# One of four token groups: turned by 32x32 blocks on VectorE through device memory, instead of by TensorE into PSUM

## The chip, the cores and the metric

The kernel runs on one core of a Trainium2 chip. A core has five engines that work side by side, each through its own queue in order: TensorE (PE in the profile; its weight loads are shown as PEld), VectorE (DVE), ScalarE (ACT), GpSimd (POOL) and SyncE (SP), which here only issues transfers. Engines wait for each other by semaphores. SBUF is the on-chip memory that transfers and engines read and write, PSUM the small one into which TensorE writes. The metric is the device time of one execution in microseconds; less is better.

## What is computed

A lightning-attention layer (causal attention with a decay per head, in blocks) for 4 sequences of 768 tokens, 8 heads of 64; its output x (4 x 768 x 512) goes through a Fourier mix and a two-layer MLP:

```python
def _moe_ref(x, w_ch1, w_ch2):
    X = np.fft.fft(x, axis=1)
    X = np.fft.fft(X, axis=2)
    mixed = np.real(X).astype(np.float32)
    u = x + mixed
    mu = np.mean(u, axis=-1, keepdims=True)
    var = np.mean((u - mu) ** 2, axis=-1, keepdims=True)
    un = (u - mu) / np.sqrt(var + 1e-06)
    ch = np.maximum(un @ w_ch1, 0.0) @ w_ch2      # 512 -> 2048 -> 512
    return (u + ch).astype(np.float32)
```

All is in fp32.

## The kernel before

**Groups.** The tokens of a sequence b are six tiles of 128. After the mix, they are handled as three groups g of two tiles each (G = 2, 256 tokens), a tile of the first half of the sequence and one of the second. `ORDER` lists the groups as they come: for each b, g = 1, 2, 0. The first four, `PLAIN` = (0, 1), (0, 2), (0, 0), (1, 1), go through the MLP by plain matrix products. The last eight, `LATE`, go through it two groups at a time at the end of the kernel, by products of combined quarter matrices (`combine_weights`, `late`), which need fewer matmuls.

**Stages.** `attn(b)` computes the attention of sequence b chunk by chunk; `fft_ln(b)` mixes it by matmuls with cosine and sine tables, adds x, and calls `norm` for each group. Beside the first two sequences the MLP's weights are loaded and decoded (`load_weights`, lines 205 to 225: the inputs are 64-bit floats, and ScalarE and VectorE make fp32 of them). `mlp(b, g, f0, f1)` does one plain group for the hidden columns f0 to f1: the first layer (line 636) into the PSUM pool pm (3 banks), relu copies to SBUF (lines 642 and 644), the second layer (line 650), then the sum with u. The first three plain groups are done in two halves of the hidden columns, all first halves (while the weights' second half is still coming) before the second halves; the fourth is done whole after them. `weave` and `beside` emit the instructions of `front` (attention and mix) and `mlp` in turns; from this order as a priority, a scheduler of the framework makes each engine's queue, with a model of durations and of free buffers. So the order on an engine is the program's order only in part.

**norm(g)**, the function that is changed: mean and variance by VectorE (546, 547), 1/sqrt by GpSimd (550, 551), then for each of the two tiles the normalised tokens `un` (563, 564), which have to be turned, so that the 512 features lie across partitions. There are two ways.
- A plain group: four TensorE transposes (569) into a PSUM tile of the pool pa (5 banks, which attention and mix use as well), and one ScalarE copy (573) into `ut`, a tile of the pool up. There are three buffers for ut, and each is free again when the second half of its group has read it for the last time.
- A late group: VectorE transposes each 32x32 block (577) into a tile of the pool ep (tag e, two buffers, shared with the weight decode's e), and four transfers on SP's queue put the blocks in their places in a device-memory tile `utd` (581). The rows u go to device memory too (587), which frees their x buffers; `late` loads both later.

A plain group's rows u stay in their x buffers until its MLP is done.

**The tail.** After `fr` and most of `back` have been emitted, `front_end.close()` gives the front's SBUF back, `combine_weights(0)` makes the combined matrices on VectorE (700), and `late` follows, four times two groups, until the end.

The lines that matter to the change: 551 to 587 (norm), 629 to 664 (mlp), 205 to 225 (the other user of e), 852 to 868 (the order of halves and the tail).

Of the kernel before, what the change touches and what calls it, by code (L numbers as in the profile page):

```python
# [76 lines left out]
def kernel(  # L77
# [10 lines left out]
    nc = tc.nc  # L88
# [8 lines left out]
    KO = DM // 128  # L97
# [5 lines left out]
    G = 2  # L103
# [14 lines left out]
    def plain_pool(name, bufs):  # L118
        return plain_end.enter_context(tc.tile_pool(name=name, bufs=bufs, side="right"))
# [9 lines left out]
    up = plain_pool("up", 3)  # L129
# [9 lines left out]
    def new(pool, shape, tag, **kw):  # L139
        cnt[0] += 1  # L140
        return pool.tile(shape, F32, tag=tag, name=f"{tag}{cnt[0]}", **kw)

    def psum_a(shape):
        return new(pa, shape, "pa")
# [265 lines left out]
    uts, utd, ud = {}, {}, {}  # L410
# [45 lines left out]
    def fold_a(b):  # L456
        for a, n in enumerate(BLK):
            yield from fold_x(b, a, n, 1, eo[b][a][1][0:n, 1, 0:DM], xn_[b, HC + a][0:n])
# [32 lines left out]
    def fft_ln(b):  # L491
        sets = []

        def piece(a, i, n):

            c0 = W + QM if i == 4 else QM * (i % 2)
            return sets[a][i in (2, 3)][0:BLK[a], n, c0:c0 + (1 if i == 4 else QM)]

        if b in LEADS:
            yield from fold_a(b)  # L500
            yield from fold_b(b, sets)
            yield 2.0
        else:
            yield 1.0
            run(fold_a(b))
            yield 6.0 if b - 1 in LEADS else 3.0
            run(fold_b(b, sets))
            yield 12.0 if b - 1 in LEADS else 9.0


        for i in range(5):
            ps = psum_a([128, 2, NK])
            m = 128 if i < 4 else 1
            for n in range(2):
                for a, rows in enumerate(BLK):
                    mm = nc.tensor.matmul(ps[0:m, n, :], lhsT=piece(a, i, n), rhs=cs[0:rows, a, i in (2, 3), n, :],  # L516
                                          start=(a == 0), stop=(a == 1))
                    if i + n + a == 0:
                        tc.keep_in_program_order(mm)
            nc.scalar.copy(ys[i][0:m, 0:2 * NK].rearrange("p (k n) -> p n k", n=2), ps[0:m])  # L520
            yield 1.4


        def width(t, ps, only_a):
            y = [ys[i][:, 128 * t:min(128 * t + 128, S // 2 + 1)] for i in range(5)]
            ps = ps[0:1] if only_a else ps
            mm = nc.tensor.matmul
            if not only_a:
                mm(ps[:, HM + QM:DM], lhsT=y[2], rhs=dt[:, 2, 0:QM], start=True, stop=True)
            mm(ps[:, HM:HM + QM + 1], lhsT=y[0], rhs=dt[:, 0, :], start=True, stop=False)  # L530
            mm(ps[:, HM:HM + QM + 1], lhsT=y[4], rhs=dt[:, 4, :], start=False, stop=True)
            mm(ps[:, 0:QM], lhsT=y[1], rhs=dt[:, 1, 0:QM], start=True, stop=True)
            if not only_a:
                mm(ps[:, QM:HM], lhsT=y[3], rhs=dt[:, 3, 0:QM], start=True, stop=True)

        def even_odd(t):
            return t.rearrange("p (m r) -> p r m", r=2)

        def halves(t):
            return t.rearrange("p (r k) -> p r k", r=2)  # L540

        def norm(g):
            mv = new(np_, [128, G, 2], "mv")
            for i in range(G):
                stt = new(np_, [128, 6], "stt")
                nc.vector.bn_stats(stt, xs[b, TT[g][i]])  # L546
                nc.vector.bn_aggr(mv[:, i, :], stt)
            ve = new(np_, [128, G], "ve")
            rs = new(np_, [128, G], "rs")
            nc.gpsimd.tensor_scalar(ve, mv[:, :, 1], EPS, None, op0=ALU.add)  # L550
            nc.gpsimd.tensor_tensor(rs, ve, mhalf, op=ALU.pow)

            yield 9.0 if (b, g) == PLAIN[0] else 1.0
            plain = (b, g) in PLAIN
            if plain:
                ut = uts[b, g] = new(up, [128, KO, G * 128], "ut")
            else:

                to = utd[b, g] = dram.tile([128, KO, G * 128], F32, name=f"utd{b}{g}")
            for i in range(G):  # L560
                un = new(np_, [128, DM], "un", bufs=1)
                u = xs[b, TT[g][i]]
                for o, x in ((un[:, 0:HM], u[:, 0:HM]), (un[:, HM:DM], u[:, DM - 1:HM - 1:-1])):
                    nc.vector.tensor_scalar(o, x, mv[:, i, 0:1], rs[:, i:i + 1],
                                            op0=ALU.subtract, op1=ALU.mult)
                if plain:
                    pt = psum_a([128, KO, 128])
                    for c in range(KO):
                        mm = nc.tensor.transpose(pt[:, c, :], un[:, 128 * c:128 * c + 128], ident)
                        if (b, g, i, c) == (*PLAIN[0], 0, 0):  # L570

                            tc.keep_in_program_order(mm)
                    nc.scalar.copy(ut[:, :, 128 * i:128 * i + 128], pt)
                else:

                    uq = new(ep, [128, DM], "e")
                    nc.vector.transpose(uq, un)
                    for r in range(0, 128, 32):
                        dst = to[:, :, 128 * i + r:128 * i + r + 32].rearrange("(a d) c n -> d c a n", d=32)
                        src = uq[r:r + 32].rearrange("p (c a n) -> p c a n", c=KO, n=32)  # L580
                        nc.sync.dma_start(dst, src)
                yield 0.7
            if plain:
                return
            for T in TT[g]:
                ud[b, T] = dram.tile([128, DM], F32, name=f"ud{b}{T}")
                nc.sync.dma_start(ud[b, T], xs.pop((b, T)))

        for t in (1, 2, 0):
            ps = psum_a([128, DM])  # L590
            width(t, ps, False)

            A = halves(ps)[:, ::-1, 0:QM]
            B = bs[t % 2]
            nc.scalar.copy(B[:, 1:HM:2], ps[:, QM:HM])
            nc.scalar.copy(B[:, 2:HM:2], ps[:, HM + QM + 1:DM])
            ds = new(fp, [128, 2 * (HM + 2)], "ds")
            nc.scalar.copy(ds[:, HM:2 * HM + 2:HM + 1], ps[:, HM + QM:HM + QM + 1].broadcast_to([128, 2]))
            nc.vector.tensor_tensor(even_odd(ds[:, 0:HM]), A, even_odd(B[:, :]), op=ALU.subtract)
            nc.vector.tensor_tensor(even_odd(ds[:, HM + 1:2 * HM + 1]), A, even_odd(B[:, :]), op=ALU.add)  # L600
            u, v_ = xs[b, t], xs[b, HC + t]
            nc.vector.tensor_tensor(halves(u), halves(u), halves(ds)[:, :, 0:HM], op=ALU.add)
            nc.vector.tensor_tensor(halves(v_), halves(v_), halves(ds[:, 1:DM + 1])[:, ::-1, :], op=ALU.add)
            yield 1.6
            if t == 0:
                ps = psum_a([128, DM])
                width(HC, ps, True)
                x3 = xn_.pop((b, HC))
                nc.vector.tensor_tensor(even_odd(v_[0:1, 0:HM]), halves(ps[0:1])[:, ::-1, 0:QM],
                                        even_odd(x3[0:1, 0:HM]), op=ALU.add)  # L610
                nc.vector.tensor_tensor(v_[0:1, HM:DM:2], ps[0:1, 0:QM], x3[0:1, HM:DM:2], op=ALU.add)
                nc.vector.tensor_tensor(v_[0:1, HM + 1:DM:2], ps[0:1, HM + 1:HM + QM + 1],
                                        x3[0:1, HM + 1:DM:2], op=ALU.add)
                yield 0.9
            yield from norm(t)
# [3 lines left out]
    PLAIN, LATE = ORDER[:4], ORDER[4:]  # L619

    def store(b, T, y, cols=slice(0, DM)):
        if T < HC:
            nc.sync.dma_start(out[b, 128 * T:128 * T + 128, cols], y[:, cols])
        else:
            nc.gpsimd.indirect_dma_start(out=out.rearrange("b s d -> (b s) d"),  # L625
                                         out_offset=row_of(2 + HC * (b + 1) + T - HC),
                                         in_=y[:, :], in_offset=None)

    def mlp(b, g, f0=0, f1=FO):

        ut = uts[b, g]
        hr = []
        for fc in range(f0, f1):
            ps = psum_m([128, G * 128])
# [186 lines left out]
    def run(gen):  # L821
        return sum(gen)
# [27 lines left out]
    run(beside(mix, 24.0, beside(att1, 2.75 * t_chunk, w, 0.16 * NW), 0.16 * NW + 1.75 * t_chunk))  # L850

    half = [[mlp(b, g, h * FO // 2, (h + 1) * FO // 2) for b, g in PLAIN[:3]] for h in range(2)]
    fr = chain([att1, fft_ln(1)] + [front(b) for b in range(2, B)])
    t_rest, t_back = 3 * t_front - 5 * t_chunk, len(PLAIN) * t_mlp - 50.0
# [51 lines left out]
```

## Time and profile before

| | us |
|---|---|
| runs: median of 4 (lowest, highest) | 822.75 (822.21, 823.99) |
| the profiled execution | 823.16 |
| its span, first to last instruction | 821.4 |
| granted TensorE clock, mean over the span | 0.998 |
| attention, mix, plain MLP and weight decode together | 0 to 430 |
| the late groups, about 97 for each two | 430 to 821.4 |

In the profile an instruction is named by engine, line and operation, with what it writes and reads (`pm<-ut,w`: a tile of pm out of ut and w). An fp32 matmul appears as two instructions, so the 64 first-layer products of a whole group, 16 by 4, appear as 128; a transpose appears once. "Idle before" is the time for which the engine stood before an instruction, with what ended it. The ends of matmuls are modelled and overlap the next one's start; the starts show the pace. In the list of windows the numbers after a stretch are its length, the busy time of PE, PEld, DVE, ACT and POOL with instruction counts, then the granted clock, the share of the transfer engines' time and GB/s.

### The profile page before, as it was taken

How to read it: one execution, taken by the hardware profiler on the slowest of the kernel's cores; microseconds unless marked ns; L12 is line 12 of the kernel's file. 1: busy time of each engine (PE TensorE's matmuls, PEld its weight loads, DVE VectorE, ACT ScalarE, POOL GpSimd, SP SyncE). 2: the span in 40 equal slices, each digit the busy share in tenths (PEclk: the TensorE clock that was granted, in tenths of full speed). 3: DMA queues.
4: the chain of work that ended last, by engine and by line, in shares of the span. 5: the costliest groups of instructions: out<-in, count | busy, mean ns of one | idle time of the engine just before them, and what ended most of it. 6: DMA issues, size and time to landing. Idle time of an engine off the chain costs nothing.

```text
span 821.4 us, 11694 instructions
## 1 busy us (share of the span) xinstructions
PE 796.2 (97%) x4608; PEld 635.8 (77%) x4608; DVE 438.0 (53%) x1018; ACT 186.3 (23%) x448; POOL 84.5 (10%) x102
## 2 busy tenths in 40 slices
PE   6889899999999999999999999999999999999998
PEld 5767767767585857768648888888888888888886
DVE  6899798766743661355895541265313661146311
ACT  3655344225420211222102200022001210022100
POOL 3123340011021010220100000000000000000000
PEclk9999999999999999999999999999999999999999
DMA  9969524249741126530351011100111001010010
GB/s 238 269 127 281 163 90 129 62 114 208 194 124 51 55 54 136 130 121 26 91 143 62 1 53 51 52 1 0 65 40 52 0 1 39 33 33 0 1 39 26
DMA packets 126684, 68.88 MB, mean 84 GB/s; under 512 B 111150, under 2 KB 112174, under 8 KB 126630
## 3 DMA queue, kind: packets, MB, share of 16 engines
q1 hardware_dynamic: 121488, 55.67, 26.7%
q0 software_dynamic: 2112, 6.69, 2.4%
q10 hardware_dynamic: 3030, 5.78, 1.9%
q8 instruction: 36, 0.59, 0.3%
q14 instruction: 18, 0.15, 0.1%
HBM read 48.72 MB, written 19.40 MB: 83 GB/s over the span
## 4 chain that ended last, share of the span: by engine, by line
PE 80%; DVE 9%; DMA 4%; issue 4%; ACT 1%; POOL 1%; SPq 0%; POOLq 0%; DVEq 0%; ACTq 0%
PE p L770 24%; PE p L723 24%; PE pm L650 10%; PE pm L636 8%; PE pa L332 3%; PE pa L516 3%; PE pa L298 2%; DMA x<-xb,ix 2%; PE pa L328 2%; DMA raw<-in_moe_w_ch_dram 1%; PE pa L274 1%; PE pa L315 1%; PE pa L348 1%; PE pa L279 1%; DVE stt L546 1%
## 5 line engine op out<-in xcount | busy, mean ns | idle before, releaser
L636 PE MATMUL pm<-ut,w 128*128 128x256 f32 x512 | 119.2, 382 | 0.0
L650 PE MATMUL pm<-w,hr 128*128 128x512 f32 x256 | 116.0, 598 | 0.2 <-DVE w L225 0.2
L636 PEld LDWEIGHTS pm<-ut,w 128*128 128x128 f32 x512 | 94.4, 190 | 15.4 <-issue 3.6
L723 PE MATMUL p<-ur,w 128*128 128x256 f32 x384 | 93.8, 379 | 0.0
L650 PEld LDWEIGHTS pm<-w,hr 128*128 128x128 f32 x256 | 46.9, 191 | 49.6 <-issue 48.1
L723 PEld LDWEIGHTS p<-ur,w 128*128 128x128 f32 x384 | 73.0, 190 | 10.3 <-issue 0.5
L723 PE MATMUL p<-us,w1s 128*128 128x256 f32 x256 | 65.7, 379 | 0.0
L770 PE MATMUL p<-w,hs 128*128 128x256 f32 x256 | 58.0, 379 | 0.5 <-DVE y L791 0.5
L770 PE MATMUL p<-w,ha 128*128 128x256 f32 x256 | 57.9, 379 | 0.0
L770 PE MATMUL p<-w2s,hs 128*128 128x256 f32 x256 | 57.9, 379 | 0.0
L770 PEld LDWEIGHTS p<-w,hs 128*128 128x128 f32 x256 | 48.5, 190 | 7.5 <-DVE y L791 0.9
L770 PEld LDWEIGHTS p<-w,ha 128*128 128x128 f32 x256 | 48.6, 190 | 6.6
L770 PEld LDWEIGHTS p<-w2s,hs 128*128 128x128 f32 x256 | 48.6, 190 | 6.6
L723 PEld LDWEIGHTS p<-us,w1s 128*128 128x128 f32 x256 | 48.6, 190 | 6.6
L625 POOL DMA_INDIRECT out_dram<-y,ix x12 | 11.8, 987 | 402.1 <-DVE y L796 342.2
L750 ACT COPY ha<-p 128x256 f32<-128x256 f32 x32 | 11.9, 372 | 169.1 <-PE p L723 139.4
L761 DVE TENSOR_TENSOR ha<-p,ha 128x256 f32<-128x256 f32 x32 | 13.6, 425 | 45.2 <-ACT ha L760 45.2
L298 PEld LDWEIGHTS pa<-qT,kT 64*128 64x128 f32 x384 | 26.0, 193 | 13.3 <-ACT qT L281 7.4
L332 PE MATMUL pa<-sc,v 128*64 128x128 f32 x384 | 32.4, 287 | 3.6 <-DVE sc L302 3.6
L302 DVE TENSOR_TENSOR sc<-pa,decay 128x512 f32<-128x512 f32 x48 | 31.5, 683 | 8.0 <-PE pa L298 7.9
L298 PE MATMUL pa<-qT,kT 64*128 64x128 f32 x384 | 30.7, 292 | 3.3 <-ACT qT L281 3.1
L270 POOL TENSOR_TENSOR kd<-k,decay 128x512 f32<-128x512 f32 x20 | 22.9, 1145 | 97.8 <-PE pa L315 49.0
(144 smaller groups left out, 1135.2 us busy)
## 6 DMA issues: line engine op xcount, KB each, us to landing
raw<-in_moe_w_ch_dram SPq DMA_DIRECT2D x32, 512.0 KB, 4.5
k<-in_k_dram SPq DMA_DIRECT2D x24, 256.0 KB, 5.1
q<-in_q_dram SPq DMA_DIRECT2D x24, 256.0 KB, 5.9
v<-in_v_dram SPq DMA_DIRECT2D x24, 256.0 KB, 4.1
ud<-x SPq DMA_DIRECT2D x16, 256.0 KB, 2.3
utd<-e SPq DMA_DIRECT2D x64, 64.0 KB, 2.2
u<-ud SPq DMA_DIRECT2D x16, 256.0 KB, 2.7
ur<-utd SPq DMA_DIRECT2D x6, 512.0 KB, 4.0
```

What stands on the lines that cost most here:

```text
L270: nc.gpsimd.tensor_tensor(kd, kt, kpow, op=ALU.mult)
L298: mm(pss[hi][:, hp, :], lhsT=kT[HD[hi], hp, :], rhs=qT[HD[hi], hp, :], start=True, stop=True)
L302: nc.vector.tensor_tensor(t, pss[hi], decay[:, hi::2, :], op=ALU.mult)
L328: mm(po[HD[hi], hp, :], lhsT=s_old[HD[hi], hp, :], rhs=qs[HD[hi], hp, :], start=(hp == 0), stop=False, skip_group_check=True)
L332: mm(po[HD[hi], hp, :], lhsT=vt[:, 2 * hp + hi, :], rhs=sc[hi][:, hp, :], start=(c == 0 and hp == 0), stop=(hp == HP - 1), skip_group_chec ...
L516: mm = nc.tensor.matmul(ps[0:m, n, :], lhsT=piece(a, i, n), rhs=cs[0:rows, a, i in (2, 3), n, :], start=(a == 0), stop=(a == 1))
L636: nc.tensor.matmul(ps, lhsT=w1[:, c, 128 * fc:128 * fc + 128], rhs=ut[:, c, :], start=(c == 0), stop=(c == KO - 1))
L650: nc.tensor.matmul(ps, lhsT=hr[(fc - f0) // 4][:, fc % 4, 128 * i:128 * i + 128], rhs=w2[:, fc, :], start=(fc == f0), stop=(fc == f1 - 1))
L723: nc.tensor.matmul(ps, lhsT=s2.A[a][:, kt, 128 * i:128 * i + 128], rhs=U[b][:, kt, :], start=(first and kt == 0), stop=(kt == 1), skip_gro ...
L750: nc.scalar.copy(a11, two(X))
L761: V.tensor_tensor(a22, two(Z), a22, op=ADD)
L770: nc.tensor.matmul(ps, lhsT=h[a][:, s, i, :], rhs=s2.B[b][:, i, :], start=(first and i == 0), stop=(i == HF - 1), skip_group_check=True)
```

## The change

The fourth plain group, (1, 1), takes the way of the late groups in `norm`: its two tiles are transposed by VectorE in blocks and written to `utd` by eight transfers. Its rows u stay in SBUF, as before (`if plain: return` is unchanged). A new function `fetch` allocates its ut and loads it from `utd` by one transfer on SP's queue; it is called at the head of the second half of group (0, 2). The other three plain groups are as before.

```diff
@@ -551,8 +551,8 @@
             yield 9.0 if (b, g) == PLAIN[0] else 1.0
-            plain = (b, g) in PLAIN
-            if plain:
+            plain, turned = (b, g) in PLAIN, (b, g) in PLAIN[:3]
+            if turned:
                 ut = uts[b, g] = new(up, [128, KO, G * 128], "ut")
             else:
@@ -563,7 +563,7 @@
                     nc.vector.tensor_scalar(o, x, mv[:, i, 0:1], rs[:, i:i + 1],
                                             op0=ALU.subtract, op1=ALU.mult)
-                if plain:
+                if turned:
                     pt = psum_a([128, KO, 128])
@@ -626,9 +626,15 @@
+    def fetch(n):
+        ut = uts[PLAIN[n]] = new(up, [128, KO, G * 128], "ut")
+        nc.sync.dma_start(ut, utd[PLAIN[n]])
+
     def mlp(b, g, f0=0, f1=FO):
 
         ut = uts[b, g]
+        if f0 > 0 and (b, g) == PLAIN[1]:
+            fetch(3)
         hr = []
```

## The prediction

> **What bounds the kernel now.** I read the page first, its busy shares and the chain of waits, then TensorE's busy time stage by stage, then the timeline around the one step that the diff touches.
>
> ```profile
> PE 796.2 (97%) x4608; PEld 635.8 (77%) x4608; DVE 438.0 (53%) x1018; ACT 186.3 (23%) x448; POOL 84.5 (10%) x102
> ...
> PE 80%; DVE 9%; DMA 4%; issue 4%; ACT 1%; POOL 1%; SPq 0%; POOLq 0%; DVEq 0%; ACTq 0%
> ```
>
> TensorE is busy for 97% of the span and holds 80% of the chain that ended last, so an instruction taken off TensorE counts, if nothing else becomes late. The windows say where it is full and where not (columns: busy us of PE, its weight loads, VectorE, ScalarE, GpSimd, then granted clock, DMA share, GB/s):
>
> ```profile
> 140.00:150.00 10.00, 9.06 (x52) 7.77 (x51) 6.05 (x14) 2.83 (x9) 0.94 (x2) 1.00 0.18 56
> ...
> 150.00:250.00 100.00, 100.00 (x673) 69.94 (x673) 64.13 (x133) 36.31 (x77) 13.70 (x16) 1.00 0.56 144
> 290.00:300.00 10.00, 8.41 (x49) 5.22 (x48) 6.15 (x17) 1.66 (x3) 2.68 (x4) 0.83 0.15 26
> 400.00:430.00 30.00, 30.00 (x78) 14.48 (x77) 28.83 (x43) 0.38 (x1) 0.93 (x2) 1.00 0.49 130
> ```
>
> From 150 to 250 us TensorE has no hole. In 140 to 150 it misses 0.94 us, and VectorE is idle for 4 of the 10. In 400 to 430 TensorE is full, and VectorE nearly so (28.83 of 30): I come back to that.
>
> **What is removed.** The fourth plain group is (1, 1). The timeline shows its eight transposes, the only ones of L569 after 117 us:
>
> ```profile
> 141.97 4.91 PE L636 MATMUL pm<-ut,w 128*128 128x256 f32 x22
> ...
> 147.82 0.76 PE L569 MATMUL pa<-ident,un 128*128 128x128 f32 x4 [0.94 <-DVE un L564]
> ...
> 148.42 1.03 PE L636 MATMUL pm<-ut,w 128*128 128x256 f32 x4
> ...
> 149.29 0.60 PE L569 MATMUL pa<-ident,un 128*128 128x128 f32 x4
> ...
> 149.72 0.39 PE L529 MATMUL pa<-dt,ys 128*128 128x128 f32 x2
> ```
>
> TensorE works in order. The run of 22 ends at 141.97 + 4.91 = 146.88; TensorE then waits 0.94 us for the normalised tokens un, with mlp matmuls ready behind the transposes. The first four take 148.42 - 147.82 = 0.60 until the next start, the second four 149.72 - 149.29 = 0.43, with no wait before them. Sum: 0.94 + 0.60 + 0.43 = **1.97 us off TensorE**. The low end, if something else at the head of the queue waits out the 0.94 instead, is 1.03. The high end counts by starts and not by ends: a matmul of L636 starts every 0.22 us but is drawn 0.38 long, so the hole is up to 0.16 longer, 2.1. I take 1.97: the next instruction behind the transposes is a matmul of L636, which needs neither un nor a bank of the pool pa.
>
> ```profile
> 246.02 1.07 ACT L573 COPY ut<-pa 128x512 f32<-128x512 f32 x2 [1.34 <-PE pm L636]
> ```
>
> The two copies out of PSUM wait for a ut buffer, and so two of pa's five banks are held from 149.3 to 247.1. Taking the copies away gives ScalarE back 1.07 + 1.34 us; TensorE runs second-layer matmuls from 245.82 to 259.7 then and waits for none of it: 0. The two banks came short without a visible price: TensorE is busy 100.00 of the 100 us in which they are held. I price them at 0, but they change what is ready when, and so the order; that is a rival below.
>
> **What is added.** Neither the group's block transposes nor its stores are in this trace, but the same lines run for the late groups:
>
> ```profile
> L577 DVE STREAM_TRANSPOSE e<-un x16: 682/704/715, 159.2 to 421.7; 128x512 f32<-128x512 f32 x16
> ...
> L581 SPq DMA_DIRECT2D utd<-e x64: 569/627/1511, 159.9 to 424.4; - x64
> ...
> DMA to landing us min/median/max: 2.1/2.2/3.7
> ```
>
> *VectorE*: two transposes, 2 x 0.704 = 1.41 us, right after the un halves, so at about 148.1 and 149.5. Covered: the next VectorE work (L599) starts at 151.57 after 2.21 us of idleness. Without that cover it would cost at most 1.4.
>
> *SP's queue*: eight stores of 64 KB, 8 x 0.627 = 5.0 us of issuing, from 148.8 to about 154.1.
>
> ```profile
> 140.21 0.33 SPq L209 DMA_DIRECT2D raw<-in_moe_w_ch_dram  x1
> 153.29 0.93 SPq L587 DMA_DIRECT2D ud<-x  x2
> 155.81 0.33 SPq L209 DMA_DIRECT2D raw<-in_moe_w_ch_dram  x1
> ```
>
> Between 140.5 and 153.29 this queue issues nothing. So the first stores of rows (ud) slip by 0.8 us, and the weight load at 155.81 not at all. At the row's longest issue, 8 x 1.511 = 12.1, that load would slip by 5 us. The last decoded weight (L225) is written at 226.3, and its half of w2 is first multiplied at 245.82: 20 us of cover, so 0 at both ends.
>
> *The slots of e*: the pool ep has two, shared by the block transposes and the weight decode. At 148 both are free: the decode's last e is read until 142 and its next one is written by ScalarE at 151.41 (L216). That one now waits for the first half's four stores: issued 148.8 to 151.3, landed 2.2 later, 153.5, so 2.1 us. Behind it on ScalarE stand the decode's next step (L218) and, for TensorE, the relu copies of L644 at 152.34 and 154.06. The three banks of pm hold three sums of 8 x 0.216 = 1.7 us each, 5.2 us of matmuls: covered, 0. With the longest rows, 4 x 1.511 and 3.7 to land, the slot is free at 158.5, ScalarE is 7.1 late, and 7.1 - 5.2 = 1.9 us of TensorE is open. I take 0: the first eight stores of the late groups, from 159.95, were through at 166.2, 6.3 us, with one long one among them (0.69, 1.51, then 0.57 to 0.63 each).
>
> [...]
>
> *The fetch*: one 512 KB load on SP, like the late groups' ur<-utd, 4.0 us to land by the page. It needs a ut buffer, which the old copies got at 246.02, and it stands at the head of the second half of group (0, 2), whose matmuls start at 261.5. The group's own first matmul is at 362.48. That is about 100 us of cover. Queued behind it is only the store of y at 253.67 if it goes out early: 0.
>
> **Does the gain reach the end?** After 430 us everything is the four-group tail, one row of matmuls. The handover is tight:
>
> ```profile
> 402.65 27.63 PE L650 MATMUL pm<-w,hr 128*128 128x512 f32 x64
> ...
> 430.12 1.89 PE L723 MATMUL p<-ur,w 128*128 128x256 f32 x8
> ...
> 430.48 0.42 DVE L661 TENSOR_TENSOR y<-pm,x 128x256 f32<-128x256 f32 x1
> 430.81 0.41 DVE L662 TENSOR_TENSOR y<-pm,x 128x256 f32<-128x256 f32 x1
> 431.23 0.37 ACT L750 COPY ha<-p 128x256 f32<-128x256 f32 x1 [29.72 <-DVE y L662]
> ```
>
> TensorE's next run (431.85) needs that copy, ended 431.60, and TensorE itself is there at 430.12 + 8 x 0.216 = 431.85. VectorE has worked without a pause from 406.04, when the weights' combining could start after the last norm. So the 1.97 us arrives only if VectorE's chain moves too. It should: it hangs on the last batch's transform (L516 at 369 to 381), behind its attention, whose last matmuls at 355 stand in TensorE's queue like all else and move with it.
>
> **Sum.** The profiled execution took 823.16 (span 821.4 and 1.76 around it). 823.16 - 1.97 + 0 = 821.19; the median of the runs shown is 0.41 below the profiled one, so **820.8**. By the bounds of the first term, and 0.5 for the measurement, this case covers 820.2 to 822.2.
>
> **Rivals.**
> *A, the gain is swallowed at 430* (0.18): VectorE's block of 406 to 431 does not move, for instance because the last batch's gathers or late stores set its start. For: 28.83 of 30 busy. Against: that chain starts from TensorE. 822.75.
>
> *B, the freed banks change the order for the better* (0.15). At 294.69 TensorE has waited 1.59 us for the score product of VectorE (L332 on L302), and in that window the clock is 0.83, 10 x 0.17 = 1.7 us more. If attention of the third batch finds five banks and this meeting falls elsewhere, 820.8 - 3.3 = 817.5. For: the scheduler has a hundred microseconds with different resources. Against: nothing says the new meeting is better.
>
> *C, slower* (0.22): the two slots of e. Three groups in a row, six halves, now pass through them between 148 and 178 beside the decode. Place: ScalarE's L216 (or VectorE's L217) at the head of its queue. It decides once ScalarE is held for more than the 5.2 us of pm. Price: the 1.9 us of the bound above, and, as after the pause at 294.69, 1.7 us of halved clock: 820.8 + 3.6 = 824.4. For: at 163.0 ScalarE already stands 2.1 us at this line, until 165.1, which is when the fourth store of a half (issued 162.91) lands, though the profile names L546. Against: TensorE lost nothing then (10.00 of 10 from 160 to 170). [...]
>
> That the change does not do what it says (the transposes or the held banks stay) I give no chance of its own: the condition that asked for the transposes and the copies no longer holds for (1, 1).
>
> **Chances and range.** The forecast has the rest, 0.45. About 0.2% (1.6 us) is what a measurement of this kernel can tell from no change, so faster means below 821.1. Of the forecast's 0.45, 0.32 lies there and 0.13 above; with B's 0.15, faster 0.47. Same is 0.13 and A's 0.16, 0.29. Slower is C's 0.22 and 0.02 of A, 0.24. The range reaches to B and C: 817.5 to 824.4, leaving out about half of each, 2 in 10.
>
> **What would show it.** No L569 after 117 us; no pause of TensorE at 147; two L577 at 148 to 150 and eight L581 before the ud stores; TensorE's tail of L723 starting at 428.1 and not 430.12, with the copy L750 two us earlier as well. A tail start at 430 with VectorE full before it is A; a window at 290 with clock 1.00 is B; a ScalarE wait at L216 above 5 us with a hole in TensorE between 150 and 180 is C. A new hole of TensorE elsewhere would make the prediction wrong in a way that I have not priced.

## The result and the profile after

The change makes the kernel slower: 825.12 us (median of 51 runs, 822.79 to 831.1) against 822.56 (77 runs, 820.35 to 828.46); the ratio is **1.0032 [1.0025, 1.004]**, 2.6 us. The forecast was 820.8. The profiled execution took 824.83, its span 823.0.

Line numbers from `mlp` on have moved by six: L636 of before is L642 here, the relu copies L644 are L650, the second layer L650 is L656, the tail's L723 is L729.

The busy share and the chain of the changed kernel, and below them its windows (columns as before):

```profile
PE 794.8 (97%) x4600; PEld 634.3 (77%) x4600; DVE 439.8 (53%) x1020; ACT 185.4 (23%) x446; POOL 86.1 (10%) x102
...
PE 77%; DVE 10%; DMA 5%; issue 3%; ACT 2%; POOL 1%; SPq 0%; DVEq 0%; POOLq 0%; ACTq 0%
```

```profile
140.00:150.00 10.00, 10.00 (x57) 9.07 (x57) 6.82 (x16) 3.80 (x13) 0.94 (x2) 1.00 0.03 14
150.00:250.00 100.00, 96.22 (x654) 67.24 (x654) 65.89 (x134) 34.84 (x72) 13.53 (x16) 0.98 0.61 155
190.00:200.00 10.00, 7.43 (x62) 6.00 (x63) 7.70 (x15) 6.71 (x14) 1.11 (x1) 0.83 1.03 252
290.00:300.00 10.00, 8.41 (x70) 5.09 (x68) 8.14 (x23) 1.07 (x2) 3.62 (x6) 1.00 0.33 57
400.00:430.00 30.00, 30.00 (x82) 15.25 (x81) 28.54 (x43) 0.38 (x1) 1.18 (x3) 1.00 0.48 121
```

TensorE has the eight transposes less (4600 matmuls for 4608) and is full from 140 to 150, where it missed 0.94. But from 150 to 250, where it had no hole, it now misses 3.78 us, and the mean clock is 0.98, not 1.00: one stretch at half clock, which costs 1.7 us (below). Most of both lies between 190 and 200. The pause at L332 that stood near 293 is still there (8.41; it now ends at 298.10), this time at full clock.

TensorE's timeline (start, length, line, instructions, idle before with what ended it) shows the gain first and the new hole 45 us later:

```profile
142.44 5.35 PE L642 MATMUL pm<-ut,w 128*128 128x256 f32 x24
147.62 0.38 PE L529 MATMUL pa<-dt,ys 128*128 128x128 f32 x2
...
186.26 4.58 PE L642 MATMUL pm<-ut,w 128*128 128x256 f32 x20 [0.75 <-ACT hr L650]
193.42 0.69 PE L274 MATMUL pa<-ident,k 128*128 128x128 f32 x4 [2.57 <-DMA k<-in_k_dram]
193.90 1.92 PE L642 MATMUL pm<-ut,w 128*128 128x256 f32 x4
```

No transpose and no wait stands at 147. From the run of L636 at 141.97 to the next L529 it took 149.72 - 141.97 = 7.75 us before, and takes 147.62 - 142.44 = 5.18 now; two instructions of the mlp fewer lie between (2 x 0.22), so 2.1 us are gained here. Then TensorE waits 0.75 us for a relu copy, and 2.57 us for the keys of the next attention chunk. The halved clock sets in with it: 4 matmuls of L642 at 193.90 take 1.71 us to the next start, 0.43 each and not 0.22.

Why the keys are late is seen on SP's queue, which issues transfers in order: after the change it issues nothing from 171.82 to 180.15, while the key load is queued behind. Before, and then after (a run of one line is drawn as one piece, pauses inside it included):

```profile
159.95 17.96 SPq L581 DMA_DIRECT2D utd<-e  x16
177.95 1.10 SPq L587 DMA_DIRECT2D ud<-x  x2
179.15 2.29 SPq L209 DMA_DIRECT2D raw<-in_moe_w_ch_dram  x2
181.53 0.38 SPq L263 DMA_DIRECT2D k<-in_k_dram  x1
```

```profile
149.33 19.29 SPq L581 DMA_DIRECT2D utd<-e  x16
168.66 1.10 SPq L587 DMA_DIRECT2D ud<-x  x2
169.86 0.40 SPq L209 DMA_DIRECT2D raw<-in_moe_w_ch_dram  x1
...
180.15 5.70 SPq L581 DMA_DIRECT2D utd<-e  x8
185.94 1.06 SPq L209 DMA_DIRECT2D raw<-in_moe_w_ch_dram  x2
187.09 0.38 SPq L263 DMA_DIRECT2D k<-in_k_dram  x1
```

Each group takes eight stores. Before, groups (1, 2) and (1, 0) are through at 177.9, and the key load k follows at 181.53. After, there are three groups; the last, (1, 0), is through only at 185.85, and the key load goes out at 187.09, 5.6 us later. (From issue to landing it takes 6.2 us, 5.8 before: the transfer itself is hardly slower.) VectorE's timeline says why (1, 0) is late; before and after, its block transposes:

```profile
171.89 0.71 DVE L577 STREAM_TRANSPOSE e<-un 128x512 f32<-128x512 f32 x1
...
173.41 0.71 DVE L577 STREAM_TRANSPOSE e<-un 128x512 f32<-128x512 f32 x1
```

```profile
148.59 0.71 DVE L577 STREAM_TRANSPOSE e<-un 128x512 f32<-128x512 f32 x1
...
150.11 0.71 DVE L577 STREAM_TRANSPOSE e<-un 128x512 f32<-128x512 f32 x1
...
174.71 0.42 DVE L663 TENSOR_TENSOR x<-pm,x 128x256 f32<-128x256 f32 x1 [7.36 <-PE pm L656]
...
178.75 0.42 DVE L217 TENSOR_SCALAR e<-raw 128x512 uint16<-128x512 uint16 x1
...
179.41 0.70 DVE L577 STREAM_TRANSPOSE e<-un 128x512 f32<-128x512 f32 x1
...
182.53 0.70 DVE L577 STREAM_TRANSPOSE e<-un 128x512 f32<-128x512 f32 x1
```

The two at 148 are the change's. The two of (1, 0) come 7.5 and 9.1 us later than before. The first has its un at 166.36, but in VectorE's queue it now stands behind other work: L663, which waits 7.36 us for TensorE, and L217 of a weight piece, the other user of e. So the shared slots act through the order that the scheduler made, more than by the landing of stores (the last store ahead of it is issued by 168.62). SP stands in front of their stores from 171.8 to 180.15 with the key load queued behind.

The tail moved with TensorE. At 431.86 the tail begins, where it was 430.12 in the execution of before:

```profile
431.86 1.89 PE L729 MATMUL p<-ur,w 128*128 128x256 f32 x8
...
432.22 0.42 DVE L667 TENSOR_TENSOR y<-pm,x 128x256 f32<-128x256 f32 x1
432.55 0.41 DVE L668 TENSOR_TENSOR y<-pm,x 128x256 f32<-128x256 f32 x1
432.97 0.37 ACT L756 COPY ha<-p 128x256 f32<-128x256 f32 x1 [29.72 <-DVE y L668]
```

The copy is again 1.1 us behind the tail's start. From there to the last matmul every profile of this study counts the same 387.34 us, so these differences arise earlier, and one measure serves for all kernels: the time from the first matmul of L529 after 137 us, just ahead of the changed place, to the first of the tail. Where a stretch of halved clock lies in it (3.41 us long in the traces of before and after, half of it lost: 1.7), the second column leaves that out; the other three profiles that have one lose 1.7 as well by the clock of their windows (0.83 over 10 us in two of them, 0.94 and 0.89 over 10 us each in the third).

| kernel | to the tail, us | without halved clock |
|---|---|---|
| before | 289.26 | 287.56 |
| after | 290.54 | 288.84 |

So by the profiles after is 1.3 us longer, with a halved stretch in both executions.

### The profile page after: what moved, and what is told of

Its sections match the earlier page's. It is cut to its first block, busy times and chain, and to the rows that moved or that the text cites. A ratio compares the mean times of both kernels' runs of the same rounds, so it can differ in the third digit from the quotient of the medians.

```text
span 823.0 us, 11693 instructions
## 1 busy us (share of the span) xinstructions
PE 794.8 (97%) x4600; PEld 634.3 (77%) x4600; DVE 439.8 (53%) x1020; ACT 185.4 (23%) x446; POOL 86.1 (10%) x102
## 4 chain that ended last, share of the span: by engine, by line
PE 77%; DVE 10%; DMA 5%; issue 3%; ACT 2%; POOL 1%; SPq 0%; DVEq 0%; POOLq 0%; ACTq 0%
PE p L776 24%; PE p L729 23%; PE pm L656 9%; PE pm L642 6%; PE pa L516 3%; PE pa L332 3%; PE pa L298 3%; DMA x<-xb,ix 2%; PE pa L328 2%; DMA raw<-in_moe_w_ch_dram 1%; DMA k<-in_k_dram 1%; PE pa L274 1%; PE pa L315 1%; PE pa L348 1%; DVE stt L546 1%
## 5 line engine op out<-in xcount | busy, mean ns | idle before, releaser
L642 PE MATMUL pm<-ut,w 128*128 128x256 f32 x512 | 120.3, 384 | 0.8 <-ACT hr L650 0.8
L656 PE MATMUL pm<-w,hr 128*128 128x512 f32 x256 | 115.6, 597 | 0.1
L642 PEld LDWEIGHTS pm<-ut,w 128*128 128x128 f32 x512 | 94.8, 191 | 16.5 <-issue 3.6
L729 PE MATMUL p<-ur,w 128*128 128x256 f32 x384 | 93.8, 379 | 0.0
L656 PEld LDWEIGHTS pm<-w,hr 128*128 128x128 f32 x256 | 46.7, 190 | 50.0 <-issue 48.5
L729 PEld LDWEIGHTS p<-ur,w 128*128 128x128 f32 x384 | 73.0, 190 | 10.3 <-issue 0.5
L729 PE MATMUL p<-us,w1s 128*128 128x256 f32 x256 | 65.7, 379 | 0.0
L729 PEld LDWEIGHTS p<-us,w1s 128*128 128x128 f32 x256 | 48.6, 190 | 6.6
L332 PE MATMUL pa<-sc,v 128*64 128x128 f32 x384 | 31.7, 282 | 4.1 <-DVE sc L302 4.0
```

The lines of the kernel that those rows point to most:

```text
L332: mm(po[HD[hi], hp, :], lhsT=vt[:, 2 * hp + hi, :], rhs=sc[hi][:, hp, :], start=(c == 0 and hp == 0), stop=(hp == HP - 1), skip_group_chec ...
L642: nc.tensor.matmul(ps, lhsT=w1[:, c, 128 * fc:128 * fc + 128], rhs=ut[:, c, :], start=(c == 0), stop=(c == KO - 1))
L656: nc.tensor.matmul(ps, lhsT=hr[(fc - f0) // 4][:, fc % 4, 128 * i:128 * i + 128], rhs=w2[:, fc, :], start=(fc == f0), stop=(fc == f1 - 1))
L729: nc.tensor.matmul(ps, lhsT=s2.A[a][:, kt, 128 * i:128 * i + 128], rhs=U[b][:, kt, :], start=(first and kt == 0), stop=(kt == 1), skip_gro ...
```

## The experiments

The expectations number three theories. 1: one meeting costs it all, TensorE with the key load that stands on SP's queue behind the held-up stores, and the halved clock after it. 2: the stores themselves, their issue time on SP and what they occupy. 3: the freed PSUM banks, which changed the order.

**The block transposes of all of sequence 1 in buffers of another pool**, so that they no longer share e with the weight decode; all 24 stores stay on SP.

```diff
-                    uq = new(ep, [128, DM], "e")
+                    uq = new(xn, [128, DM], "xn") if b == 1 else new(ep, [128, DM], "e")
```

> The changed kernel, but the block-transposed halves of the second sequence (b = 1) go into the two free buffers of the pool xn instead of the two slots of e that the weight decode uses. Theory 1 (slots): the stores of the late group (1, 0) came 7.5 us later (180.2 instead of 172.6) because a weight piece took the e slot ahead of them, and so they stood in front of the third chunk's key load (187.1 instead of 181.5), for which TensorE waited 2.6 us and then ran at half clock. With own slots these stores are out before 178, the key load before 183, TensorE does not wait for it, and the time is 2 us under the kernel before (ratio 0.9976). Theory 2 (issue time): what counts is that SP issues 24 stores of some 0.63 us instead of 16; the key load stays about 5 us late and the ratio at 1.003. Theory 3 (freed banks): the two free banks let attention ask for the keys 2 us earlier; the wait stays at about 2 us or more, ratio 1.001 to 1.003.

820.45 us, ratio 0.9993 [0.9975, 1.0011]; to the tail 285.69. SP's queue:

```profile
149.46 17.12 SPq L581 DMA_DIRECT2D utd<-xn  x16
...
168.31 9.73 SPq L581 DMA_DIRECT2D utd<-xn  x8
...
181.80 0.38 SPq L263 DMA_DIRECT2D k<-in_k_dram  x1
```

The block transposes of (1, 0) on VectorE, 12.4 and 13.1 us earlier than in the change:

```profile
167.03 0.70 DVE L577 STREAM_TRANSPOSE xn<-un 128x512 f32<-128x512 f32 x1
...
169.42 0.70 DVE L577 STREAM_TRANSPOSE xn<-un 128x512 f32<-128x512 f32 x1
```

With the same 24 stores on the same queue the last is out at 178.04, the keys leave when they did before, and TensorE doesn't wait for them; a wait of 0.9 us for a ScalarE copy (L281) remains. The stores' issue time alone is not the cause of the late keys; the lateness that the shared slots bring is. The time is only back at that of before: the forecast of 0.9976 lies at the edge of the interval.

**The group's eight stores on ScalarE's queue.**

```diff
-                        nc.sync.dma_start(dst, src)
+                        (nc.scalar if plain else nc.sync).dma_start(dst, src)
```

> The changed kernel, but the eight stores of the group (1, 1) are issued from ScalarE's queue instead of SP's; slots of e as in the change. Theories 1 and 2: SP's order is that of the kernel before or better, the third chunk's key load goes out at 182 or earlier, no wait of TensorE at 190; the ratio is 0.9976 unless ScalarE, which issues for 8 x 0.63 = 5 us at 149 to 154, holds up the relu copies (then up to 1.000). Theory 3: the wait for the keys does not hang on these stores and stays; ratio 1.001 to 1.003.

818.82 us (817.36 to 821.75), ratio **0.996 [0.9946, 0.9973]**, to the tail 285.08: faster than either kernel. The two queues:

```profile
148.01 5.46 ACTq L581 DMA_DIRECT2D utd<-e  x8
```

```profile
155.27 0.38 SPq L263 DMA_DIRECT2D k<-in_k_dram  x1
155.74 0.53 SPq L263 DMA_DIRECT2D q<-in_q_dram  x1
...
161.87 18.43 SPq L581 DMA_DIRECT2D utd<-e  x16
```

The third chunk's keys now go out ahead of the late groups' stores, 32 us sooner than in the change; TensorE's largest wait for a load is 0.3 us. ScalarE is held for 5.5 us at 148, and TensorE loses nothing by it (busy 20.00 of the 20 us from 140 to 160). The eight moved stores are not the late ones. Without them on SP the order of the queues came out otherwise: the block transposes of (1, 0), 179.41 and 182.53 in the change, stand at 173.57 and 176.23. So the gain is that of a new order, and not the price of eight issues on SP.

**Only the third chunk's three loads on ScalarE's queue**, the stores as in the change.

```diff
-            nc.sync.dma_start(t, src[b, :, rows, :].rearrange("h p d -> p h d"))
+            (nc.scalar if (b, c) == (2, 2) else nc.sync).dma_start(t, src[b, :, rows, :].rearrange("h p d -> p h d"))
```

> The changed kernel, but the third chunk's loads of k, q and v of sequence 2 are issued from ScalarE's queue, so that they do not stand behind the stores. All three theories say that the wait of 2.6 us at TensorE's transposes of k and the half clock after it go; what is left is the gain of the transposes: ratio 0.9976 (819 to 821.5 us). If the ratio stays at 1.003, the key load was only named by the profile, and the loss comes from somewhere else (the freed banks' order, or the weight decode that is late as well).

820.45 us, ratio 0.9991 [0.9974, 1.0008], to the tail 286.05. The key wait and the halved clock are gone; this remains of the list of waits of TensorE (in all, times, longest):

```profile
PE pm L642 <- ACT hr L650: 1.0, 1, 1.0
PE pa L298 <- ACT qT L281: 0.8, 2, 0.5
```

The load is the bigger part: 825.12 - 820.45 = 4.7 us by the medians, 3.4 by the two ratios, and by the profiles 2.8 (288.84 - 286.05) and the halved stretch, 1.7.

**The change without its stores.** The eight stores of the group are left out, and its fetch reads another group's tile.

```diff
-                        nc.sync.dma_start(dst, src)
+                        if not plain:
+                            nc.sync.dma_start(dst, src)
...
-        nc.sync.dma_start(ut, utd[PLAIN[n]])
+        nc.sync.dma_start(ut, utd[LATE[0]])
```

> The changed kernel without the eight stores of the group (1, 1); its tokens are fetched from the tile of the late group (1, 2) instead, so the output rows of (1, 1) are another group's MLP. VectorE's transposes, the fetch and the freed banks stay. Theories 1 and 2: SP's order and the slots of e are those of the kernel before, no wait for the keys, ratio 0.9976. Theory 3: the banks are as free as in the change, attention asks for the keys as early, the wait stays at about 2 us: 1.001 to 1.003.

819.18 us, ratio 0.9964 [0.9947, 0.998], to the tail 284.48. The key load goes out at 180.10 and no wait for it is left, though the banks are as free as in the change: theory 3 falls. And 287.56 - 284.48 = 3.1 us is what the removal is worth while the stores are not paid for.

**The transposes kept on TensorE, the banks freed**: each half is copied to an SBUF buffer at once, written by one plain store and fetched later like in the change.

```diff
-                if turned:
+                if plain:
...
-                    nc.scalar.copy(ut[:, :, 128 * i:128 * i + 128], pt)
+                    if turned:
+                        nc.scalar.copy(ut[:, :, 128 * i:128 * i + 128], pt)
+                    else:
+                        uc = new(xn, [128, DM], "xn").rearrange("p (c n) -> p c n", c=KO)
+                        nc.scalar.copy(uc, pt)
+                        nc.sync.dma_start(to[:, :, 128 * i:128 * i + 128], uc)
```

> The group (1, 1) is turned by TensorE as before, but each half is copied out of PSUM at once into a free buffer of the pool xn and kept in device memory (one store for each half), and fetched as in the change: the banks are freed, TensorE's transposes stay, VectorE's do not come, SP gets 2 stores instead of 8, e is untouched. If the gain seen without the key wait comes from the transposes taken off TensorE (the prediction's 1.97 us) and the banks are worth nothing, this is the time before: ratio 0.999 to 1.001. If the gain comes from the freed banks, ratio 0.996 to 0.998. In either case no wait for the keys at 190.

820.24 us, ratio 0.9981 [0.9966, 0.9996], to the tail 287.07. The ratio lies between the two forecasts. The freed banks, with the two copies moved away from 246, are no loss. By the profiles they are worth 287.56 - 287.07 = 0.5 us, hardly more than three profiles of the order of before differ among themselves (287.25 to 287.62); by the times 0.0019, 1.6 us, with an interval from 0.3 to 2.8. The remaining 287.07 - 284.48 = 2.6 are the transposes and their pause, 2.1 at their place as shown above, and 0.5 that arise later and are put down to nothing here.

**The suspect added to the kernel before**: the group is turned by TensorE as before, and its halves are also block-transposed and stored, for nobody to read.

```diff
                     nc.scalar.copy(ut[:, :, 128 * i:128 * i + 128], pt)
+                    if (b, g) == PLAIN[3]:
+                        uq = new(ep, [128, DM], "e")
+                        nc.vector.transpose(uq, un)
...
+                            nc.sync.dma_start(dst, src)
```

> The kernel before, which also block-transposes the group (1, 1) on VectorE into e and sends its eight stores through SP to a device-memory tile that nobody reads: the cost alone, without the gain. Theory 1 (the loss is one late key load that TensorE meets): what counts is whether the third chunk's key load lands before TensorE's transposes of it, at 192.5 in the kernel before, 2 us later than in the change. If it goes out by 185 it costs nothing: ratio 0.999 to 1.001; if the stores of (1, 0) fall behind a weight piece as in the change and it goes out at 187, 1 to 3 us: 1.001 to 1.004. Theory 2 (24 stores on SP cost as such): the loss without the gain, 4.7 us, ratio 1.005 to 1.006.

826.92 us, ratio **1.0071 [1.0051, 1.0091]**, to the tail 293.06. Its waits of TensorE, and one window:

```profile
PE pa L274 <- DMA k<-in_k_dram: 2.9, 1, 2.9
```

```profile
190.00:200.00 10.00, 7.09 (x40) 5.73 (x40) 8.94 (x18) 6.85 (x14) 3.23 (x1) 0.83 1.02 265
```

The transposes and stores alone bring the key wait (the load leaves at 187.63) and the halved clock. Theory 1 had put it at 1.001 to 1.004: it had counted the wait and neither the clock nor the next experiment's remainder. Theory 2's 1.005 to 1.006 lies in the interval, though the wait and the clock that theory 1 names are there.

**The same, with the third chunk's loads on ScalarE's queue** (both edits above).

> The kernel before with the added block transposes and eight unread stores of (1, 1), as in before_blocks (+5 us there), but with the third chunk's loads of k, q and v of sequence 2 issued from ScalarE's queue. Theory 1 (all of the added cost is the late key load that TensorE meets, and the halved clock after it): 822 again, ratio 0.998 to 1.002. Theory 2 (24 stores on SP and the shared slots cost as such, also by late weight pieces): at least 2 us stay, ratio 1.0025 or more.

824.08 us, ratio 1.003 [1.0017, 1.0043], to the tail 289.43; no key wait, no halved clock. Of the 5 us that the stores had added, about 3 were the key load with its clock (826.92 - 824.08 = 2.8, by the ratios 3.4) and about 2 remain (289.43 - 287.56 = 1.9, a wait of 1.0 for a relu copy among them). For that remainder theory 2 is right.

**The kernel before with that move alone.**

> A control: the kernel before with only the third chunk's loads of k, q and v of sequence 2 moved to ScalarE's queue. In the kernel before TensorE does not wait for these keys, so by theory 1 nothing is gained: ratio 0.998 to 1.001. If it is as fast as the changed kernel with the same move (0.9976), the move helps by something else and says nothing of the change.

821.83 us, ratio 0.9998 [0.9989, 1.0007]: where the keys are in time, moving their load is worth nothing.

**Own slots and ScalarE's queue together.**

> Both remedies together: the block-transposed halves of the second sequence in the free buffers of xn, and the eight stores of (1, 1) issued from ScalarE's queue. Theory 1: no wait for the keys, ScalarE no longer waits for slots of e; not slower than with the stores alone moved (818.8): ratio 0.995 to 0.997.

820.8 us, ratio 0.9995 [0.9979, 1.0011]: a miss, this was to be as good as the stores on ScalarE alone. The profile has another meeting (TensorE's timeline):

```profile
174.19 0.60 PE L642 MATMUL pm<-ut,w 128*128 128x256 f32 x2
177.13 1.16 PE L298 MATMUL pa<-qT,kT 64*128 64x128 f32 x16 [2.34 <-ACT qT L281]
178.22 2.40 PE L642 MATMUL pm<-ut,w 128*128 128x256 f32 x6
```

The order of the work came out differently, TensorE waits for ScalarE's copy of the queries, and the clock halves again (6 matmuls in 2.33 us). Two edits that each take the key wait away do not add up.

**The stores on ScalarE's queue and the third chunk's loads there too.**

> The change with both moves: the eight stores of (1, 1) and the third chunk's loads of k, q and v from ScalarE's queue. The key load is no longer late with the stores alone moved (818.8), so by theory 1 nothing more is to be had: ratio 0.995 to 0.997. Another number shows what a new order costs or brings.

818.89 us, ratio 0.9963 [0.9951, 0.9975], to the tail 284.54, leaving out a halved stretch behind the pause at L332: nothing beyond the stores' move.

**The kernel before once more.**

> The kernel before again, for a second profile: the pause of 1.6 us at TensorE's wait for the score product near 293 should be there again, since the order is the same; whether the clock is halved after it again is open. If it is not, that 1.7 us belongs to the execution and not to the kernel.

822.9 us, 1.0012 [0.9999, 1.0026], to the tail 287.62. The pause of 1.6 us near 293 is there (now ending at 294.38), and the clock in that window is 1.00:

```profile
290.00:300.00 10.00, 8.41 (x54) 4.61 (x53) 7.21 (x19) 1.56 (x3) 2.68 (x4) 1.00 0.16 28
```

The halved stretch of the first profile belongs to that execution and not to the kernel.

## Why the prediction was wrong

*The gain* of 1.97 us was right: TensorE gains 2.1 at that place, the high end that the prediction had counted by starts. Over the whole way to the tail the removal gives up to 3.1 (without the stores); the other 1.0 is in part the banks, priced at 0 (0.5 by the profiles), and in part not assigned. *ScalarE's copies* at 0, *VectorE's two transposes* under cover (148.59 and 150.11) and *the fetch* (issued at 249.31, used at 364.28) were as said. *The handover at 430* lets gains through: the tail starts at 425.07 with the stores on ScalarE and at 425.26 without stores. Rival A falls; in rival B the clock near 293 was no property of the kernel, as the second profile of before showed, and the pause itself stayed.

**The step that failed is SP's queue**, "the weight load at 155.81 not at all ... so 0 at both ends". The issuing was sized rightly (149.33 to 154.7 for 148.8 to 154.1). But only the weight loads were followed down the queue. The load that TensorE meets next, k of the third chunk at 181.53, stands in the same queue behind two more groups' stores, and I took these to stay where they were. They didn't: SP's queue stood from 171.8 to 180.15 at a store whose data were late, and everything behind it stood too. Keys at 187.09 instead of 181.53, with a TensorE that comes earlier by its gain, make the 2.57 us. It is the "new hole of TensorE elsewhere" that the prediction had named and not priced.

**The slots of e**, "I take 0", at most 1.9, are the other half of the same step. Rival C had the sign, the time (824.4 for 825.12) and the halved clock; its path, ScalarE's relu copies, is real but gives 0.75 us of TensorE. That its number came close is luck. The slots cost more by delaying (1, 0)'s block transposes by 7.5 us, and those hold SP. Both are needed: with other slots the keys are in time on SP, and with the same slots they are in time on another queue.

The sum as the runs give it, relative to before and without the clock: -3.1 for what was removed, +1.6 for slots and stores with the keys out of the way (286.05 - 284.48), +2.8 for the key wait (288.84 - 286.05): +1.3. (It has to come out as 288.84 - 287.56, being made of the same column.) Measured is +2.6.

The rest fits the halved clock, 1.7 us for a stretch: it followed the long pause (2.6 and 2.9 us) in both profiles that have the key wait, and the pause at 293 in one of the two profiles of before. How often it comes is on record too, in each execution's mean granted clock. A stretch takes 1.7 of some 822 us, so a mean of 0.998 or below is read as one or more of them: 42 of 53 executions of the changed kernel have it, and 33 of the 84 of before that were measured beside the experiments. One minus the mean, times the span, averages 2.2 us for the changed kernel and 0.95 for before. That is 1.2 more, and 1.3 + 1.2 = 2.5 of the 2.6. The means are rounded to 0.001, 0.8 us, so this is an estimate.

What stays open: which part of the 1.6 is a slot, which the stores' traffic and which the new order of the work. With other slots 1.2 of it stayed (285.69 - 284.48), with a different wait in it.

## What to carry to other kernels

When a step puts transfers on an in-order queue, follow that queue to the next load that the bounding engine needs, however many entries behind, and ask of every entry in between whether its data will still be ready when they were. A buffer pool shared by two producers makes that answer change. A load that the bounding engine needs soon does not belong behind stores whose producer may be late. With the load alone on another queue the loss of 2.6 us was gone, though nothing was gained (ratio 0.9991, its interval holds 1). Where the queues' order came out with the load ahead of the late stores, 3.3 us were gained (822.43 x 0.004, by its own comparison); but own slots with the same eight stores on ScalarE's queue (0.9995) show that such a gain can't be counted on.

## What the hardware showed unasked

Here a pause well under the length of a halved stretch brought one at times. The pause of 1.6 us at L332 stands in the profiles of all kernels here; in 2 of 13, before and both moves to ScalarE's queue, the clock halved after it (0.83 over the 10 us from 290 in both; 3.41 us at half in the trace of before). After the three pauses of 2.3 to 2.9 us (the change, the blocks added to before, own slots with ScalarE's queue) it halved each time (0.83 over the 10 us from 190 in the first two, 0.72 over the 6 us from 178 in the third). It is not certain even so: 11 of the 53 executions of the changed kernel have a mean clock of 0.999 or 1.000, too high for a whole stretch (whether their pause was as long is not on record). At the cost of 1.7 us these pauses are priced too low by their length alone.

In the traces of before and after the halved stretch is 3.413 us long. From its start (295.55 and 193.86) to the next drop of the clock, behind the last matmul (821.20 and 821.91), it is 525.65 and 628.05 us, 154.0 and 184.0 times that length. What sets the start of a stretch is not shown by this.

Eight strided stores of 64 KB cost ScalarE's queue 5.46 us of issuing (0.68 each), much as on SP's (5.39 in the kernel before with blocks added).
